# RetNet attention and a top-2 expert layer on one core: where evacuations, fetches and a loop count are issued

## The chip, the core and the metric

The kernel runs on one core of a Trainium2 chip. A core has five engines that run their own instruction queues in order: TensorE (PE; its weight loads are shown as PEld), VectorE (DVE), ScalarE (ACT), GpSimd (POOL) and SyncE (SP, which here only issues DMAs). They wait for one another through semaphores. Matmul results land in PSUM and must be copied ("evacuated") to SBUF by DVE or ACT before the PSUM buffer can be used again. The metric is the device time of one execution in microseconds (us), as a median of runs. All times below are in us unless marked ns, and places in the run are given from the start of the span, which reaches from the first to the last instruction.

## The reference

Attention with a decay in place of a softmax feeds a mixture of eight experts of which each token takes two.

```
scores = scale * q @ k.T                      # q, k, v: (8, 8, 576, 64)
ret    = scores * Dmat                        # Dmat: gamma_h ** (i - j) for i >= j, else 0
attn   = ret @ v
x = attn.transpose(0, 2, 1, 3).reshape(4608, 512)
logits = x @ w_gate + log1p(exp(x @ w_noise)) * noise
top2, weights = the two largest logits of a token, softmax over the two
out[token] = sum over its two experts of weight * (relu(x @ w1[e]) @ w2[e])   # w1: 512x1024, w2: 1024x512
```

## The kernel before

**Attention** works in 16 units. Unit u is one batch and four heads; two batches (bp) make four units. 512 of the 576 positions are done with 128-wide tiles, and the last 64 ("the tail") of two batches together. The methods of the class Attention (the main loop's order in a unit is scores for hp 0, out, tr of q, scores for hp 1, cast and tr of k, scores_tail, states and out_tail, with one step() behind each of these seven):
- scores(u, hp) (L248): 16 matmuls of keys and queries into two PSUM tiles "S" (two buffers), then the evacuation: DVE multiplies them with the causal mask into two tiles S in bf16 (L263). It is called for hp 0 and hp 1.
- out(p) (L290) for the unit before: 32 matmuls of S with the values (L305) and 6 with the carried states and queries (L313) into two PSUM tiles "x"; one is copied to xT by ACT (L321) and one by DVE (L319).
- tr(u+1, "q") and tr(u+1, "k") (L228): 8 transposes each into PSUM "tr" (two buffers, shared with the router's row copies), and a copy by ACT to QT or KT (L244).
- cast(u+2) (L185): POOL scales k and q into kn (L192) and qb (L200), ACT casts v (L197).
- scores_tail, states(u) (L266: 32 matmuls into PSUM "T", one buffer, copied by ACT to Tb, L285), out_tail.

**The router** is a Python generator, route(bp) (L469), for the tokens of two batches. It is cut into pieces by yield. The inner function step() of the main function runs one piece; the main loop calls it seven times a unit, between the calls above, so that a piece's instructions stand in every engine's queue between those of attention. One route spreads over four units. Its pieces are: the logits matmuls (L489) and the first row of x (transposes L482, copy L483); the logits to SBUF (lg, L496 and L497) and exp and ln of the noise part on ACT (L499, L500, with an ACT table load); noise and the first maximum (L515 to L525); the second maximum; the choice M, running counts cum on POOL (L549) and exp of the difference d (L553); gates, ranks and flags (L558 to L636); one-hot products olo and oh on DVE (L643 to L652, two halves); two groups of nine matmuls R (L663), one for each half; then the table of slots (L667 and finish(), L690 to L693), a matmul of counts (L681), and the end. The rows of x go to DRAM as xd (L626).

**The early tiles.** When three routes are done, early() (L354) starts on five tiles of expert work, again piece by piece, beside the last route: gathers on POOL (L370), transposes (L383), first and second matmuls (L392, L402).

**The experts.** experts() handles the other 35 tiles of 256 tokens (LATE, expert by expert). The order of instructions is written out by hand. In iteration i: the results of tile i-1 that are a token's first expert are scaled and stored to yd (fin); tile i+2 is transposed (L931, copied by ACT L934); the second matmuls of tile i (L966) are issued two by two with the first matmuls of tile i+1 (L947), whose evacuations to hT alternate between ACT (L952) and DVE (L954); comb(i-1), issued behind the second of these evacuations, adds the scaled result of tile i-1 to prv, which holds the rows of yd from the token's other expert (L1002). Then, on POOL: gathers of tile i+5 (L828), and for each half s of a tile the scatter of tile i-1 to out (L1008) and the fetch prev(i+1, s) of rows of yd (L974). Last come casts and loads of weights. The second matmuls run over the contraction index outside and the two halves inside, so both halves of a tile end together. prv has four buffers.

**The end.** After all scatters POOL copies keep["nov"], the number of overflow tiles, to keep["nov2"] (L1055); this copy waits for every row of out. overflow() then loads that count into a register of each engine (L739) and enters a loop (L740), which runs as often as the count says.

Of the kernel before, what the change touches and what calls it, by code (L numbers as in the profile page):

```python
# [9 lines left out]
F32 = mybir.dt.float32  # L10
# [119 lines left out]
class Attention:  # L130
# [3 lines left out]
    def __init__(self, tc, ctx, raw, K, q, k, v):  # L134
        self.tc, self.nc, self.K = tc, tc.nc, K
        self.src = dict(q=q, k=k, v=v)
        nc = self.nc
        ep = lambda n, b, **kw: ctx.enter_context(tc.tile_pool(name=n, bufs=b, **kw))
        self.cp = ep("at_c", 1)
        self.raw = raw  # L140
        self.bf = ep("at_bf", 2)
        self.tp = ep("at_t", 2)
        self.sp = ep("at_s", 2)
        self.xp = ep("at_x", 2)
        self.ps = ep("at_ps", 1, space=bass.MemoryType.PSUM)
        self.Tb = [self.cp.tile([P, 2, 4, P], BF16, name=f"Tb{j}") for j in range(4)]
        self.u = {}
        self.tails = {}
        self.T = {}
        self.xT = {}  # L150

    @staticmethod
    def unit(u):

        return u // 4, u // 2 % 2, u % 2

    def tables(self):
# [90 lines left out]
    def scores(self, u, hp):  # L248
        nc = self.nc
        d = self.u[u]  # L250
        p = [self.ps.tile([P, 2, 2, P], F32, name="S", bufs=2) for h in range(2)]
        for c in range(2):
            for r in range(2):
                for h in range(2):
                    s = slice(h * HD, (h + 1) * HD)
                    for e in range(2):
                        nc.tensor.matmul(p[h][e * HD:(e + 1) * HD, c, r, :],  # L257
                                         lhsT=d["K"][s, hp, c, r, e, :],
                                         rhs=d["Q"][s, hp, 2 * c + e, :],
                                         start=(c == 0 and r == 0), stop=(c == 1 and r == 1), skip_group_check=True)  # L260
        for h in range(2):
            S = self.sp.tile([P, 2, 2, P], BF16, name=f"S{hp}{h}")
            nc.vector.tensor_tensor(S, p[h], self.K["mask"].unsqueeze(1).to_broadcast([P, 2, 2, P]), Alu.mult)  # L263
            d["S", hp, h] = S

    def states(self, u):  # L266
# [15 lines left out]
        T = self.Tb[u % 4]  # L282
        for h in range(2):
            s = slice(h * HD, (h + 1) * HD)
            nc.scalar.activation(T[s, :, :, s].rearrange("p y n d -> p (y n) d"),  # L285
                                 p[s].rearrange("p y n d -> p (y n) d"), Act.Copy)
        for hp in range(2):
            d["T", hp] = self.T[bp, b, 2 * hq + hp] = T[:, hp]

    def out(self, u):  # L290
# [17 lines left out]
        for e in range(2):  # L308
            for hp in range(2):
                for c in range(2):  # L310
                    j = 2 * c + e
                    if j:
                        nc.tensor.matmul(p[e][:, hp, c, :],  # L313
                                         lhsT=d["T", hp][:, j - 1, :], rhs=d["Q"][:, hp, j, :], start=False,
                                         stop=(hp == 1 and c == 1), skip_group_check=True)
            xv = self.xT[bp][:, 2 * hq:2 * hq + 2, 4 * b:4 * b + 4, :].rearrange(
                "p y (c e) t -> p y c e t", e=2)[:, :, :, e, :]
            if e:
                nc.vector.tensor_copy(xv, p[e])  # L319
            else:  # L320
                nc.scalar.activation(xv, p[e], Act.Copy)  # L321

# [109 lines left out]
class Router:  # L432
# [36 lines left out]
    def route(self, bp):  # L469
# [26 lines left out]
        V.tensor_copy(lg, pg[:, :, 1])  # L496
        V.tensor_add(lg, lg, pg[:, :, 0])  # L497
        nl = sp.tile([P, C, E], F32, name="nl")
        nc.scalar.activation(nl, lg[:, :, E:], Act.Exp)  # L499
        nc.scalar.activation(nl, nl, Act.Ln, bias=1.0)  # L500
        yield
        row(1)
# [48 lines left out]
        d = col("d")  # L551
        V.tensor_sub(d, m2, m1)  # L552
        nc.scalar.activation(d, d, Act.Exp)  # L553
        yield

# [102 lines left out]
        G.tensor_tensor(key, key, ov, Alu.mult)  # L658
        G.tensor_scalar(key, key, -1.0, None, Alu.add)
        pT = ps.tile([P, 2 * NH], F32, name="R", bufs=1)  # L660
        for j in range(2):
# [70 lines left out]

def overflow(tc, K, w1, w2, keep, xd, yd, out):

    nc = tc.nc
    V = nc.vector
    with tc.tile_pool(name="ov_c", bufs=1) as cp, tc.tile_pool(name="ov_o", bufs=4) as op, \
         tc.tile_pool(name="ov_ps", bufs=1, space=bass.MemoryType.PSUM) as ps:
        n = nc.values_load(keep["nov2"][0:1, 0:1], min_val=0, max_val=NOV)  # L739
        with tc.For_i(0, n, 1) as iv:  # L740
            kb = cp.tile([P, 1], F32, name="kb")
            V.tensor_copy(kb, keep["ovk"][:, bass.ds(iv, 1)])
            e = nc.gpsimd.value_load(keep["ove"][0:1, bass.ds(iv, 1)], min_val=0, max_val=E - 1)
# [89 lines left out]
def experts(tc, K, wp, w1, w2, keep, xd, yd, out, W, pre):  # L833
# [7 lines left out]
    with tc.tile_pool(name="moe_g", bufs=1) as gp, \  # L841
# [117 lines left out]
        def g2(i):  # L959
            w = W[LATE[i][0]]  # L960
            hT = st[i]["hT"]
            po = [ps.tile([P, DM], F32, name="po", bufs=4) for s in range(2)]
            for fi in range(KF):
                for s in range(2):
                    o = KD * F + fi * DM
                    nc.tensor.matmul(po[s], lhsT=hT[:, fi, s * P:(s + 1) * P], rhs=w[:, o:o + DM],  # L966
                                     start=(fi == 0), stop=(fi == KF - 1))
                    yield
            st[i]["po"] = po

        def prev(i, s):
            if i < NT and seconds(i)[s]:
# [3 lines left out]
                    in_offset=IOff(ap=st[i]["ix"][:, s, 1:2], axis=0),  # L976
                    bounds_check=rows - 1, oob_is_err=False)

        def fin(i):
# [35 lines left out]
        with tc.manual_schedule(engines=order):  # L1015
# [9 lines left out]
            for _ in g1(0, {}):  # L1025
                pass
            wload(0)
            for i in range(NT + 1):
                if i:
# [14 lines left out]
                for s in range(2):  # L1044
                    if i + 5 < NT:
                        gather(tc, keep, xd, xgof(i + 5), i + 5, s)
                for s in range(2):
                    if i and seconds(i - 1)[s]:
                        scat(i - 1, s)
                    prev(i + 1, s)  # L1050
                st.pop(i - 1, None)
                wcast(i)
                wload(i + 1)

        last = nc.gpsimd.tensor_copy(keep["nov2"], keep["nov"]).ins  # L1055
        for w in writes:
# [15 lines left out]
def kernel(  # L1072
# [20 lines left out]
    keep = dict(z=cp.tile([P, NH], F32, name="z"), xi=cp.tile([P, NH], I32, name="xi"),  # L1093
                key=cp.tile([P, 2, NCOL], F32, name="key"), nov=cp.tile([P, 1], I32, name="nov"), nov2=cp.tile([P, 1], I32, name="nov2"),
                ovk=cp.tile([P, NOV], F32, name="ovk"), ove=cp.tile([P, NOV], I32, name="ove"))
# [4 lines left out]
    with ExitStack() as actx, tc.manual_schedule(engines=order):  # L1100
# [131 lines left out]
```

## Time and profile before

| what | us |
|---|---|
| median of 6 runs | 580.49 (578.16 to 584.46) |
| the profiled execution | 578.05 |
| its span | 576.3 |
| PE busy | 450.2 (78%) |
| DVE busy | 272.6 (47%) |
| ACT busy | 275.1 (48%) |
| POOL busy | 287.0 (50%) |
| mean granted TensorE clock | 0.858 of full speed |

A busy share is a mean over stretches with different limits, so the run is best read in stretches: loading and the first units (0 to 48), attention with routes (48 to 186), the last route with the early tiles (186 to 245), the experts (245 to 557), and the end. In the lines of the profile a group is named by its line in the kernel, engine, operation and tiles (out<-in), and the bracket holds the idle time of the engine just before it and what ended that. "issue" stands for idle time that the profile cannot lay to another engine.

### The profile page before, as it was taken

Reading aid. Unit: us, or ns where it says so; the run is one execution under the profiler, and the core shown is the slowest. Engines: PE = TensorE matmul, PEld = TensorE weight load, DVE = VectorE, ACT = ScalarE, POOL = GpSimd, SP = SyncE. Lnnn points to the kernel's source line nnn. Section 1 sums busy time; section 2 is a strip of 40 time slices with the busy share of each in tenths; the row PEclk is TensorE's granted clock in tenths of the full one; section 3 lists DMA queues with packets and bytes.
Section 4 is the critical chain, followed back from the end, with each engine's and each line's share of the span. In section 5 each row is a group of like instructions: output and inputs, shape, how many; then the busy total and the mean of one; then the engine's idle time right before and its main releaser. Section 6 shows DMA issues by size and latency. Waiting matters only on the chain.

```text
span 576.3 us, 11679 instructions
## 1 busy us (share of the span) xinstructions
PE 450.2 (78%) x4587; PEld 312.9 (54%) x4627; DVE 272.6 (47%) x696; ACT 275.1 (48%) x413; POOL 287.0 (50%) x377
## 2 busy tenths in 40 slices
PE   1697776884783799689996996997996997898960
PEld 1576554663562566466662663664563664465630
DVE  5354997698577485333231351341332333243430
ACT  4686963782581585436553652753452642212200
POOL 4962495278333555721464055157067165576470
PEclk9987775676686799799996998998799899899995
DMA  9976999606717224636684676667565643443350
GB/s 262 346 187 185 288 347 279 201 28 136 125 32 149 76 83 150 190 138 221 208 276 151 208 242 203 222 238 235 200 221 179 225 145 118 140 144 124 126 183 20
DMA packets 96169, 104.19 MB, mean 181 GB/s; under 512 B 25447, under 2 KB 73064, under 8 KB 96112
## 3 DMA queue, kind: packets, MB, share of 16 engines
q1 hardware_dynamic: 79824, 69.51, 38.0%
q0 software_dynamic: 14176, 32.83, 20.4%
q10 hardware_dynamic: 2112, 1.08, 0.6%
q8 instruction: 37, 0.61, 0.4%
q14 instruction: 20, 0.16, 0.1%
HBM read 84.66 MB, written 28.72 MB: 197 GB/s over the span
## 4 chain that ended last, share of the span: by engine, by line
PE 35%; issue 22%; DVE 16%; POOL 10%; DMA 7%; SPq 4%; ACT 2%; another core or an unknown queue 1%; POOLq 0%; DVEq 0%; ACTq 0%
PE p L947 12%; PE po L966 10%; POOL xg L828 4%; DVE S L263 3%; SPq L174 2%; PE S L392 2%; DMA xg<-xd,xi 2%; DMA raw_k<-in_k_dram 2%; PE x L402 2%; POOL prv L974 2%; DMA raw_q<-xd,xi 2%; POOL out_dram L1008 2%; DVE olo L643 1%; PE T L279 1%
## 5 line engine op out<-in xcount | busy, mean ns | idle before, releaser
L947 PE MATMUL p<-xgT,w 128*128 128x256 bf16 x1120 | 222.6, 282 | 22.1 <-issue 15.7
L966 PE MATMUL po<-w,hT 128*128 128x512 bf16 x525 | 204.1, 393 | 9.5 <-issue 7.0
L947 PEld LDWEIGHTS <-w 128*128 128x128 bf16 x1120 | 112.5, 101 | 102.6 <-issue 35.9
L954 DVE TENSOR_SCALAR hT<-p 128x512 bf16<-128x512 f32 x70 | 48.3, 691 | 195.2 <-PE p L947 119.2
L952 ACT ACTIVATE hT<-p 128x512 bf16<-128x512 f32 x70 | 41.8, 598 | 171.1 <-PE p L947 63.7
L1008 POOL DMA_INDIRECT out_dram<-o,ix x45 | 45.6, 1013 | 114.2 <-DVE o L1002 100.0
L828 POOL DMA_INDIRECT xg<-xd,xi x64 | 65.8, 1028 | 19.2 <-issue 17.4
L966 PEld LDWEIGHTS <-hT 128*128 128x128 bf16 x560 | 55.9, 100 | 23.4 <-issue 15.3
L974 POOL DMA_INDIRECT prv<-yd,ix x45 | 46.0, 1023 | 36.1 <-DMA wst<-in_moe_w_dram 22.7
L263 DVE TENSOR_TENSOR S<-S,mask 128x512 bf16<-128x512 f32 x64 | 41.1, 684 | 32.8 <-PE S L257 32.6
L897 ACT ACTIVATE w<-wst 128x1024 bf16<-128x1024 f32 x48 | 47.9, 1050 | 0.0
L192 POOL TENSOR_TENSOR kn<-raw_k,kg 128x1024 bf16<-128x1024 f32 x14 | 27.2, 1940 | 29.3 <-PE T L279 15.4
L934 ACT ACTIVATE xgT<-pt 128x1024 bf16<-128x1024 bf16 x35 | 35.7, 1020 | 2.2 <-PE pt L931 2.2
L1002 DVE SCALAR_TENSOR_TENSOR o<-po,g,prv 128x512 f32<-128x512 f32 x45 | 31.7, 743 | 3.0 <-DMA prv<-yd,ix 3.0
L200 POOL TENSOR_TENSOR qb<-raw_q,qg 128x1024 bf16<-128x1024 f32 x14 | 30.3, 2165 | 0.0
L257 PE MATMUL S<-QT,KT 64*64 64x128 bf16 x512 | 19.1, 278 | 10.3 <-DVE S L263 7.1
L549 POOL TENSOR_TENSOR cum<-cum,M 128x16 bf16<-128x16 bf16 x36 | 8.1, 226 | 36.5 <-DVE d L552 34.0
L242 PE MATMUL tr<-ident,qb 128*128 128x128 bf16 x128 | 15.3, 292 | 12.8 <-DVE qb L200 12.8
L279 PE MATMUL T<-vn,kn 64*64 64x64 bf16 (+2 forms) x512 | 25.3, 243 | 0.0
L482 PE MATMUL tr<-ident,xT 128*128 128x128 bf16 x144 | 17.6, 260 | 9.5 <-ACT QT L244 7.5
L483 ACT ACTIVATE xr<-tr 128x512 bf16<-128x512 bf16 x36 | 21.4, 597 | 4.6 <-issue 2.9
L931 PE MATMUL pt<-ident,xg 128*128 128x128 bf16 x256 | 20.7, 219 | 3.0 <-issue 2.5
(210 smaller groups left out, 659.0 us busy)
## 6 DMA issues: line engine op xcount, KB each, us to landing
wst<-in_moe_w_dram SPq DMA_DIRECT2D x48, 512.0 KB
raw_k<-in_k_dram SPq DMA_DIRECT2D x32, 256.0 KB
raw_v<-in_v_dram SPq DMA_DIRECT2D x32, 256.0 KB
yd<-y SPq DMA_DIRECT2D x16, 512.0 KB
raw_q<-in_q_dram SPq DMA_DIRECT2D x14, 512.0 KB
xd<-xr SPq DMA_DIRECT2D x12, 396.0 KB
w<-in_moe_w_dram POOLq DMA_DIRECT2D x4, 1024.0 KB
yd<-raw_v SPq DMA_DIRECT2D x5, 512.0 KB
```

The source lines that it names most:

```text
L263: nc.vector.tensor_tensor(S, p[h], self.K["mask"].unsqueeze(1).to_broadcast([P, 2, 2, P]), Alu.mult)
L279: nc.tensor.matmul(p[h * HD:(h + 1) * HD, hp, n, :], lhsT=d["kn"][:k, r, c, 2 * hp + h, :], rhs=m, start=(c == 0 and k == P and r == 0 and ...
L828: tc.nc.gpsimd.indirect_dma_start(out=xg[:, s, :], out_offset=None, in_=xd[:, :], in_offset=IOff(ap=keep["xi"][:, j:j + 1], axis=0), bound ...
L897: nc.scalar.activation(W[e][:, k * F:(k + 1) * F], t, Act.Copy)
L934: return lambda: nc.scalar.activation(xgT, pt, Act.Copy)
L947: nc.tensor.matmul(p1[:, f2, :], lhsT=w[:, o:o + P], rhs=xgT[:, di, :], start=(di == 0), stop=(di == KD - 1))
L952: nc.scalar.activation(hT[:, 2 * fp:2 * fp + 2, :], p1, Act.Relu)
L954: V.tensor_relu(hT[:, 2 * fp:2 * fp + 2, :], p1)
L966: nc.tensor.matmul(po[s], lhsT=hT[:, fi, s * P:(s + 1) * P], rhs=w[:, o:o + DM], start=(fi == 0), stop=(fi == KF - 1))
L974: nc.gpsimd.indirect_dma_start(out=prv[i % NP][:, s, :], out_offset=None, in_=yd[:rows, :], in_offset=IOff(ap=st[i]["ix"][:, s, 1:2], axis=0),
L1002: V.scalar_tensor_tensor(o[:, s, :], st[i]["po"][s], st[i]["g"][:, s:s + 1], prv[i % NP][:, s, :], Alu.mult, Alu.add)
L1008: ins = nc.gpsimd.indirect_dma_start(out=out[:, :], out_offset=IOff(ap=st[i]["ix"][:, s, 0:1], axis=0), in_=st[i]["o"][:, s, :], in_offset ...
```

## The change

It has these parts.
1. The evacuations in scores, states and out are put into small functions, kept in a list self.late, and issued by flush(), which step() calls after the router piece. So the evacuation of a call stands behind the router piece that follows it, in the queues of DVE and ACT. Both copies of xT are issued together. scores_tail, out_tail and tr are as before.
2. In route, two yields move: the one behind exp and ln of the noise part now stands ahead of them, and the one behind exp of d now stands ahead of it. One yield is added ahead of the two R groups, so a route has one piece more.
3. In experts, the fetches of y of a tile are issued up to two tiles ahead (i+2 in iteration i), both halves together and ahead of the scatters, as soon as stored() says that all tiles whose rows they can read have had their stores issued.
4. In the last tile the second matmuls run half by half: all eight of the first half, then all eight of the second.
5. The loop count is read ahead of experts(), straight from keep["nov"]; the copy that waits for the rows of out now copies keep["ovk"] (96 columns) to keep["ovk2"], which the loop reads.

```diff
@@ class Attention
+    def flush(self):
+
+        for f in self.late:
+            f()
+        self.late.clear()
@@ scores
-        for h in range(2):
-            S = self.sp.tile([P, 2, 2, P], BF16, name=f"S{hp}{h}")
-            nc.vector.tensor_tensor(S, p[h], self.K["mask"].unsqueeze(1).to_broadcast([P, 2, 2, P]), Alu.mult)
-            d["S", hp, h] = S
+
+        def take():
+            for h in range(2):
+                S = self.sp.tile([P, 2, 2, P], BF16, name=f"S{hp}{h}")
+                nc.vector.tensor_tensor(S, p[h], self.K["mask"].unsqueeze(1).to_broadcast([P, 2, 2, P]), Alu.mult)
+                d["S", hp, h] = S
+        self.late.append(take)
@@ states: the copies to T likewise
...
@@ out
-            xv = self.xT[bp][:, 2 * hq:2 * hq + 2, 4 * b:4 * b + 4, :].rearrange(
-                "p y (c e) t -> p y c e t", e=2)[:, :, :, e, :]
-            if e:
-                nc.vector.tensor_copy(xv, p[e])
-            else:
-                nc.scalar.activation(xv, p[e], Act.Copy)
+
+        def take():
+            xv = self.xT[bp][:, 2 * hq:2 * hq + 2, 4 * b:4 * b + 4, :].rearrange("p y (c e) t -> p y c e t", e=2)
+            nc.scalar.activation(xv[:, :, :, 0, :], p[0], Act.Copy)
+            nc.vector.tensor_copy(xv[:, :, :, 1, :], p[1])
+        self.late.append(take)
@@ route
         V.tensor_add(lg, lg, pg[:, :, 0])
+        yield
         nl = sp.tile([P, C, E], F32, name="nl")
         nc.scalar.activation(nl, lg[:, :, E:], Act.Exp)
         nc.scalar.activation(nl, nl, Act.Ln, bias=1.0)
-        yield
         row(1)
...
         V.tensor_sub(d, m2, m1)
+        yield
         nc.scalar.activation(d, d, Act.Exp)
-        yield
...
         G.tensor_scalar(key, key, -1.0, None, Alu.add)
+        yield
         pT = ps.tile([P, 2 * NH], F32, name="R", bufs=1)
@@ overflow
-        n = nc.values_load(keep["nov2"][0:1, 0:1], min_val=0, max_val=NOV)
         with tc.For_i(0, n, 1) as iv:
             kb = cp.tile([P, 1], F32, name="kb")
-            V.tensor_copy(kb, keep["ovk"][:, bass.ds(iv, 1)])
+            V.tensor_copy(kb, keep["ovk2"][:, bass.ds(iv, 1)])
@@ experts, g2
-            for fi in range(KF):
-                for s in range(2):
+
+            for fi, s in ((fi, s) for fi in range(KF) for s in range(2)) if i + 1 < NT else (
+                    (fi, s) for s in range(2) for fi in range(KF)):
@@ experts
+        def stored(i, n):
+
+            return i >= NT or all(j < n for j in range(NT) if LATE[j][0] < LATE[i][0] and any(firsts(j)))
...
+            pv = 0
             for i in range(NT + 1):
...
+                while pv <= i + 2 and stored(pv, i):
+                    for s in range(2):
+                        prev(pv, s)
+                    pv += 1
                 for s in range(2):
                     if i and seconds(i - 1)[s]:
                         scat(i - 1, s)
-                    prev(i + 1, s)
...
-        last = nc.gpsimd.tensor_copy(keep["nov2"], keep["nov"]).ins
+        last = nc.gpsimd.tensor_copy(keep["ovk2"], keep["ovk"]).ins
@@ main function, step
                     work.append(early(tc, K, at, keep, xd, yd, W, EARLY, routed))
+            at.flush()
             if n == NU:
                 more()
@@ main function, end
+    nov = nc.values_load(keep["nov"][0:1, 0:1], min_val=0, max_val=NOV)
     experts(tc, K, wp, moe_w1, moe_w2, keep, xd, yd, out, W, pre)
-    overflow(tc, K, moe_w1, moe_w2, keep, xd, yd, out)
+    overflow(tc, K, moe_w1, moe_w2, keep, xd, yd, out, nov)
```

More of the change, by code (lines that the diff above doesn't have):

```diff
@@ L146, in __init__ @@
         self.Tb = [self.cp.tile([P, 2, 4, P], BF16, name=f"Tb{j}") for j in range(4)]
+        self.late = []
         self.u = {}
@@ L282, in states @@
         T = self.Tb[u % 4]
[L283 to L286, printed above, removed]
+        def take():
+            for h in range(2):
+                s = slice(h * HD, (h + 1) * HD)
+                nc.scalar.activation(T[s, :, :, s].rearrange("p y n d -> p (y n) d"),
+                                     p[s].rearrange("p y n d -> p (y n) d"), Act.Copy)
+        self.late.append(take)
         for hp in range(2):
@@ L315, in out, with take @@
                                          stop=(hp == 1 and c == 1), skip_group_check=True)
-            xv = self.xT[bp][:, 2 * hq:2 * hq + 2, 4 * b:4 * b + 4, :].rearrange(
-                "p y (c e) t -> p y c e t", e=2)[:, :, :, e, :]
-            if e:
-                nc.vector.tensor_copy(xv, p[e])
-            else:
-                nc.scalar.activation(xv, p[e], Act.Copy)
+        def take():
+            xv = self.xT[bp][:, 2 * hq:2 * hq + 2, 4 * b:4 * b + 4, :].rearrange("p y (c e) t -> p y c e t", e=2)
+            nc.scalar.activation(xv[:, :, :, 0, :], p[0], Act.Copy)
+            nc.vector.tensor_copy(xv[:, :, :, 1, :], p[1])
+        self.late.append(take)
     def scores_tail(self, bp, hq):
@@ L730, in overflow_list, with overflow @@
         V.scalar_tensor_tensor(keep["ovk"], self.K["iota"][:, :NOV], float(P), ei, Alu.mult, Alu.add)
-def overflow(tc, K, w1, w2, keep, xd, yd, out):
+def overflow(tc, K, w1, w2, keep, xd, yd, out, n):
     nc = tc.nc
@@ L1093 @@
     keep = dict(z=cp.tile([P, NH], F32, name="z"), xi=cp.tile([P, NH], I32, name="xi"),
-                key=cp.tile([P, 2, NCOL], F32, name="key"), nov=cp.tile([P, 1], I32, name="nov"), nov2=cp.tile([P, 1], I32, name="nov2"),
+                key=cp.tile([P, 2, NCOL], F32, name="key"), nov=cp.tile([P, 1], I32, name="nov"), ovk2=cp.tile([P, NOV], F32, name="ovk2"),
                 ovk=cp.tile([P, NOV], F32, name="ovk"), ove=cp.tile([P, NOV], I32, name="ove"))
```

## The prediction

> **What bounds the kernel now.** I read the page first (its share by engine and its chain), then the busy times by stretch, then the waits of each engine in the attention stretch, then the timelines at the places that these named. All times are microseconds from the start of the span. The span is 576.3, the profiled execution took 578.05, so 1.75 lie around it; the median of the runs shown is 580.49, which is 2.44 above the profiled execution. I make the sum against 578.05 and add the 2.44 at the end.
>
> ```profile
> 48.00:186.00 138.00, 96.12 (x1721) 75.44 (x1720) 107.75 (x249) 79.94 (x119) 71.47 (x105) 0.67 0.69 175
> 245.00:300.00 55.00, 52.31 (x391) 36.49 (x397) 19.10 (x57) 28.43 (x38) 18.22 (x19) 0.99 0.61 209
> 480.00:557.00 77.00, 69.04 (x473) 44.72 (x481) 32.06 (x81) 19.79 (x29) 45.90 (x46) 0.98 0.41 134
> 557.00:576.30 19.30, 0.00 (x0) 0.00 (x0) 1.06 (x2) 0.00 (x0) 4.03 (x5) 0.58 0.20 70
> ```
>
> Columns are the stretch, its length, busy time of PE, PEld, DVE, ACT and POOL, the granted clock, DMA share and GB/s. There are three regimes. From 48 to 186 attention and router share the engines: DVE is busy 78%, no engine is full, so waits between engines decide. From 245 to 557 PE is full (95% in the first of the two stretches shown): there the order of DMAs on POOL costs nothing unless PE runs dry. From 557 PE is done and POOL's queue alone sets the end. So the change is worth something in the first regime and the last.
>
> ```profile
> PE R L663 <- DVE oh L652: 14.8, 6, 4.6
> PE tr L482 <- ACT QT L244: 7.5, 3, 2.9
> PE S L257 <- DVE S L263: 6.9, 4, 3.2
> ```
>
> These are PE's three longest waits of 48 to 186 (total, times, longest). The first two are the router's pieces getting into attention's way, and the change moves both.
>
> **Evacuations behind the router piece: the end of a group.** Four units of attention carry one route. A group takes 48 to 49 (the lg copies stand at 57.08, 105.05 and 154.09). At its end the second half of the one-hot products is made while PE waits in order for it:
>
> ```profile
> 138.25 1.65 DVE L650 TENSOR_TENSOR oh<-oh,cols 128x720 bf16<-128x720 bf16 x1
> 139.94 1.95 DVE L652 TENSOR_SCALAR oh<-oh,pidx 128x720 bf16<-128x720 bf16 x1
> 141.94 1.36 PE L663 MATMUL R<-oh,olo 128*128 128x160 bf16 x9 [4.65 <-DVE oh L652]
> 143.23 0.64 PE L257 MATMUL S<-QT,KT 64*64 64x128 bf16 x16
> 143.91 1.29 DVE L263 TENSOR_TENSOR S<-S,mask 128x512 bf16<-128x512 f32 x2 [1.43 <-PE S L257]
> 145.48 0.17 PE L681 MATMUL R<-cum,ones 128*128 128x16 bf16 x1 [1.61 <-DVE L L667]
> ```
>
> Read it downward: DVE ends its product at 141.89, PE does the second R group, then the score matmuls, DVE idles 1.43, and PE waits again 1.61 before the transposes of kn. In the changed instruction lists R moves one piece later (the new yield), so the scores of the unit's second half stand before that second R, and the S evacuation of the first half stands behind the products. DVE has the same work up to 141.89, in another order. Then: scores at 141.9 to 142.2 (they follow the freed buffers), R 1.36 to 143.5, transposes of kn at 143.5 instead of 145.50; the counts matmul falls behind them and no longer stalls. That is 2.0 a group. From 146 to 154 PE runs without a gap over 0.3, so the 2.0 stay. Two groups end with scores behind them (at 94 and 142; the first shows the same wait, 4.38); the third has none. **Gain 4.0.**
>
> **Yields moved in the router's first pieces.** Before, ScalarE's table load stood ahead of the QT copy:
>
> ```profile
> 154.76 0.26 ACT L499 ACTIVATE nl<-lg 128x72 f32<-128x72 f32 x1 [1.11 <-DVE lg L497]
> 155.04 1.28 ACT L500 ACT_TABLE_LOAD   x1
> 156.50 1.01 ACT L244 ACTIVATE QT<-tr 128x1024 bf16<-128x1024 bf16 x1
> 157.56 0.58 PE L482 MATMUL tr<-ident,xT 128*128 128x128 bf16 x4 [2.88 <-ACT QT L244]
> ```
>
> After, QT is first (154.15, when its transposes end, to 155.17), then exp, table load and ln (0.26+1.28+0.26, to 156.97), then the xr copy of 0.6 to 157.55; the kn transposes, which need that copy's buffer, come at 157.55 instead of 158.05. So 2.88 of wait is worth only 0.5: the wait moves from the row's transposes to kn's. Three groups: **1.5**. This adds a wait: the nl product now stands in the next DVE slot, waits for ln until 157.0, and the S evacuation of 154.72 stands behind it, until 157.6 to 158.9. Who waits for that? The next scores, at 160.99; they do not, by 2.1. The exp of d moves likewise; its load (113.89) already ran in a pause of ACT. DVE then fills the 0.42 for which it waits for PE before the xT copy (114.35 and 163.66) with the 0.65 of pd and thr: 0.4 twice, **0.8**. The Tb copies go behind a row copy of 0.6; their reader (L313) comes 2.7 after the copy's end (149.92 to 152.62), so nothing.
>
> **The start of the early tiles.** One more piece per route makes early begin one step later, and the instruction lists have the tail's products and the first logits matmuls (1.01 and 0.72) ahead of its first transposes. These waited 4.11 for a gather (184.56 to 188.67), so 1.7 of PE work goes into that wait. What is late next is the copy to raw_v (190.58 to 191.6), beside which the next 16 logits matmuls and a row (0.63 and about 0.4) stand. The second R of the last route has the same number of early pieces ahead of it as before. **1.7.**
>
> **The experts.** The pairs of fetches of y now go out one tile earlier and ahead of the scatters; their number is the same (45 at 1.02 each). POOL's queue behind a fetch that waits for its stored rows holds the scatters and then the gathers. Before, one fetch waited 22.7 (248.4 to 271.1) and PE stood nowhere over 0.5 between 251 and 302: a gather is issued two whole tiles before its transposes, some 15 at 7.6 a tile (379.63 to 387.21). Later the scatters themselves wait for DVE up to 22.5, so POOL is ahead. **0**, with up to 7 lost if one 22.7 wait came back where POOL leads by only 15 (its wait at 357 and at 403).
>
> **The end.**
>
> ```profile
> 555.52 1.03 POOL L974 DMA_INDIRECT prv<-yd,ix  x1 [0.30 <-issue]
> 559.05 0.75 DVE L1002 SCALAR_TENSOR_TENSOR o<-po,g,prv 128x512 f32<-128x512 f32 x1 [1.74 <-DMA prv<-yd,ix]
> 560.78 0.98 POOL L1008 DMA_INDIRECT out_dram<-o,ix  x1 [0.30 <-issue]
> 563.74 0.19 POOL L1055 COPY nov<-nov 128x1 int32<-128x1 int32 x1 [1.97 <-DMA out_dram<-o,ix]
> ```
>
> From 551.54 POOL issues eight DMAs, one each 1.31; the last two fetches lie between. After, the order is six scatters: 551.54, 552.86, then 554.93 (its o starts at 553.93, first half 0.7, handover 0.3), 556.25, 557.57, 558.88. The o of the last tile's first half can start at 555.4, since with halves in order its 8 matmuls end at about 554.9; the second half's o runs from 556.9 to 557.65. The last scatter is at 558.88 instead of 560.78: **1.9**. By scatter spacing alone it would be 2.6, without the halves about 1.2.
>
> The loop count: the lists show the load moved only on SP. On PE, ACT, DVE and POOL it still stands last, and POOL's own comes behind the copy, which still waits for every row of out. What it waits for is done earlier, but POOL's queue is what ends. Gain 0 (at best the 0.5 of one load). SP now waits for nov (230.68) between two stores of y; at most 1, and the weights behind it went out at 238.04. The copy is 96 wide instead of 1: rows near it are 0.17 (128x24) and 0.56 (128x528 memset), I take 0.1 **lost**.
>
> **Sum.** 4.0 + 1.5 + 0.8 + 1.7 + 1.9 - 0.1 = 9.8. 578.05 - 9.8 = 568.25, and on the median 570.7.
>
> **Two costs that the trace of before cannot fix.** First, the same DVE instruction takes 1.75 or 0.23 (L602), 1.95 or 0.43 (L652), 1.77 or 0.18 (L636), the long ones whenever POOL casts kn or qb beside it, and S evacuations do not stretch. A new order meets other casts: one collision of 1.5 more or less in each of three groups, so 4.5 either way; I take 0. [...] Second, the granted clock was 0.50 from 133.3 to 153.8. If PE's shorter waits released it, the 8 of full PE work from 146 to 154 could shrink by up to half, 4 a group; the clock can equally stay, so 0 is taken. [...]
>
> **Rivals.**
> (1) Bonus: as forecast, and collisions or the clock give 4 to 9 more: 562 to 567. For it: S evacuations, which do not collide, now face the second cast. Against: DVE, not PE, is bound from 116 to 142. Chance 0.16.
> (2) Given back: the new wait behind ln (2.9 in three groups, 8.7) is paid, and eats the 8.0 of attention and start; 1.8 at the end remain: about 579.4. It decides if the next scores come less than 2.9 after the old evacuation's end; the row says 5.0 (156.0 to 160.99). Chance 0.17.
> (3) Slower: every S evacuation behind a router piece is waited for by PE's next scores, since there are two buffers. Pieces ahead in a group: 2.9 (nl), 0.8 (w, M), 0.9 (r, df), 1.2 (rki to ov), 0.9 (oh), 1.3 (the products), 8.0, three groups 24.0, less 9.8: 594.7. It decides where the delay passes the spare time between an evacuation and the next scores: 2.2 (113.77 to 115.94) and 4.3 (117.86 to 122.18), but nothing where PE already waits 2.92 (131.75), where DVE is the bound anyway. Chance 0.15.
> (4) The change not doing what it says concerns the loop count alone, and is in the sum at 0.
>
> **How the numbers follow.** The forecast, 570.7, has 0.52; its own range is 564 to 577. With rival 1 that is 0.68 for faster by over 0.5% (below 577.6); 0.5% is about what a measurement of this kernel can tell from no change. Within: 0.17. Slower: 0.15. The range of 8 in 10 runs from 562 (9.8, 4.5 and 4 all gained) to 582 (rival 2 with 2.6 of collisions) and leaves out rival 3.
>
> **What would show it.** Right: no PE wait of over 2 at L663's second group of the first two routes; QT ahead of the table load; groups of 45 to 46.5; stretch 245 to 557 as long as before; six scatters at the end. Wrong: S evacuations with PE's scores waiting for them over 10 in total; a fetch of y waiting over 15; a later last scatter in relation to the last matmul.

## The result and the profile after

The changed kernel takes **586.35** in the median of 20 runs (583.64 to 593.47), the kernel before 580.57 (46 runs). The ratio is 1.0095, with a 95% interval of 1.0075 to 1.0114: about 1% slower, where 570.7 was forecast and 582 was the range's end. The profiled execution took 585.19, its span 583.5.

Line numbers from the class Attention on are 7 to 22 higher in the changed kernel: L263 is L272 there, L257 L264, L244 L251, L523 L536, L652 L665, L663 L677, L1008 L1026.

Busy time by stretch, after (columns as in the prediction):

```profile
48.00:186.00 138.00, 95.44 (x1794) 75.57 (x1795) 108.13 (x242) 83.34 (x125) 65.81 (x105) 0.71 0.75 179
245.00:300.00 55.00, 48.16 (x360) 34.51 (x366) 15.91 (x47) 28.57 (x38) 16.77 (x17) 0.91 0.60 206
557.00:583.50 26.50, 8.83 (x53) 5.04 (x52) 5.43 (x8) 1.19 (x2) 6.13 (x7) 0.74 0.17 66
```

From 245 to 300 PE is busy 48.16 in place of 52.31, since the experts begin later (their first xgT copy stands at 251.0 in place of 240.6); in the last row PE still works after 557. So everything stands later, and the time is lost before the experts. PE's longest waits from 48 to 186, after:

```profile
PE S L264 <- DVE S L272: 21.1, 15, 6.5
PE S L264 <- ACT KT L251: 5.7, 2, 3.9
PE tr L249 <- ACT xr L496: 5.3, 3, 1.8
...
PE R L677 <- DVE oh L665: 1.3, 2, 1.1
PE tr L495 <- ACT QT L251: 1.1, 2, 0.5
```

The two waits that the change was to remove are gone (R from 14.8 to 1.3, row transposes from 7.5 to 1.1). The wait for QT moved to the transposes of kn, which wait for the xr copy (5.3), as forecast. But the waits for S evacuations went from 6.9 to 21.1; over 10 was to speak against the forecast. The end of a group shows the exchange (timeline, after):

```profile
140.39 1.28 DVE L272 TENSOR_TENSOR S<-S,mask 128x512 bf16<-128x512 f32 x2
141.12 0.32 PE L264 MATMUL S<-QT,KT 64*64 64x128 bf16 x2 [4.75 <-DVE S L272]
...
148.90 0.43 DVE L665 TENSOR_SCALAR oh<-oh,pidx 128x720 bf16<-128x720 bf16 x1
149.24 1.27 DVE L272 TENSOR_TENSOR S<-S,mask 128x512 bf16<-128x512 f32 x2
149.97 0.32 PE L264 MATMUL S<-QT,KT 64*64 64x128 bf16 x2 [2.72 <-DVE S L272]
...
151.13 1.38 PE L677 MATMUL R<-oh,olo 128*128 128x160 bf16 x9
```

The second R group (151.13) now waits for nothing, but the scores wait 4.75 and 2.72 for evacuations that stand behind router pieces, and 4.65 was the wait removed.

To see where the rest lies, I cut each span at four landmarks: the first lg copy (loads and first units), the first xgT copy of the experts, the last xgT copy, and the end. These are the profiles that the text below uses, all from one execution each ("aligned" means that tiles keep their place within 256 bytes, "no deferral" that evacuations are issued at once; both are told below):

| kernel | to first lg | to first xgT | experts | end | span |
|---|---|---|---|---|---|
| before | 57.1 | 183.5 | 301.2 | 34.6 | 576.3 |
| after | 60.7 | 190.3 | 299.9 | 32.6 | 583.5 |
| e1 attention as before | 64.9 | 183.5 | 298.3 | 33.0 | 579.7 |
| e5 before, shifted by 352 bytes | 64.3 | 180.9 | 302.5 | 34.6 | 582.3 |
| e6 after, aligned | 56.0 | 185.7 | 289.5 | 33.0 | 564.2 |
| e7 no deferral, aligned | 56.9 | 178.1 | 288.4 | 32.9 | 556.3 |
| e8 attention as before, aligned | 59.5 | 184.5 | 293.1 | 33.3 | 570.5 |
| e16 before, shifted by 512 bytes | 58.8 | 180.9 | 253.5 | 34.6 | 527.8 |
| e14 as e7 | 58.1 | 174.0 | 252.6 | 33.2 | 517.8 |
| e17 as e6 | 54.8 | 180.1 | 253.0 | 33.3 | 521.2 |

Against before, the changed kernel loses 3.6 at the start and 6.8 in attention, and gains 1.3 in the experts and 2.0 at the end. From e13 on every kernel was 45 to 49 quicker, the kernel before too (528 in place of 577; told last), so each result is given as a ratio to the kernel before measured beside it.

### The profile page after: what moved, and what is told of

The parts are those of the page before. It is cut to its first block, busy times and chain, and to the rows that moved or that the text cites. A ratio compares the mean times of both kernels' runs of the same rounds, so it can differ in the third digit from the quotient of the medians.

```text
span 583.5 us, 11684 instructions
## 1 busy us (share of the span) xinstructions
PE 451.4 (77%) x4587; PEld 312.9 (54%) x4627; DVE 274.0 (47%) x696; ACT 274.9 (47%) x413; POOL 279.0 (48%) x377
## 4 chain that ended last, share of the span: by engine, by line
PE 52%; DVE 18%; issue 10%; DMA 6%; SPq 5%; ACT 3%; another core or an unknown queue 3%; POOL 1%; POOLq 0%; DVEq 0%; ACTq 0%
PE p L960 23%; PE po L980 19%; DVE S L272 3%; DMA raw_v<-in_v_dram 3%; PE pt L944 3%; SPq L181 3%; PE S L405 2%; PE x L415 2%; SPq L188 2%; DVE olo L656 1%; DVE o L1020 1%; DVE oh L663 1%; DVE oh L660 1%; PE R L677 1%
## 5 line engine op out<-in xcount | busy, mean ns | idle before, releaser
L1026 POOL DMA_INDIRECT out_dram<-o,ix x45 | 45.6, 1013 | 113.8 <-DVE o L1020 99.9
L272 DVE TENSOR_TENSOR S<-S,mask 128x512 bf16<-128x512 f32 x64 | 41.1, 683 | 31.9 <-PE S L264 31.6
L264 PE MATMUL S<-QT,KT 64*64 64x128 bf16 x512 | 20.3, 268 | 28.2 <-DVE S L272 21.3
L947 ACT ACTIVATE xgT<-pt 128x1024 bf16<-128x1024 bf16 x35 | 35.7, 1019 | 5.5 <-PE p L960 3.2
L264 PEld LDWEIGHTS <-KT 64*64 64x64 bf16 x512 | 12.8, 130 | 33.5 <-issue 23.8
L207 POOL TENSOR_TENSOR qb<-raw_q,qg 128x1024 bf16<-128x1024 f32 x14 | 28.1, 2005 | 0.0
L204 ACT ACTIVATE vn<-raw_v 128x1024 bf16<-128x1024 f32 x16 | 16.9, 1056 | 17.6 <-DMA raw_v<-in_v_dram 11.8
L249 PE MATMUL tr<-ident,qb 128*128 128x128 bf16 x128 | 13.8, 273 | 12.8 <-DVE qb L207 12.8
L496 ACT ACTIVATE xr<-tr 128x512 bf16<-128x512 bf16 x36 | 21.1, 596 | 4.4 <-PE tr L495 2.7
```

The source lines that it names most:

```text
L264: nc.tensor.matmul(p[h][e * HD:(e + 1) * HD, c, r, :], lhsT=d["K"][s, hp, c, r, e, :], rhs=d["Q"][s, hp, 2 * c + e, :], start=(c == 0 and ...
L947: return lambda: nc.scalar.activation(xgT, pt, Act.Copy)
L1026: ins = nc.gpsimd.indirect_dma_start(out=out[:, :], out_offset=IOff(ap=st[i]["ix"][:, s, 0:1], axis=0), in_=st[i]["o"][:, s, :], in_offset ...
```

## The experiments

**Which part loses.** Theory A: the new wait for ln is paid (rival 2). Theory B: every S evacuation behind a piece is late (rival 3). Theory C: the loss has to do with neither. e1 undoes the attention and router parts (the two xT copies stay together), e2 only the deferral:

```diff
-        self.late.append(take)     # e1, e2: in scores, states and out
+        take()
```

> The changed kernel with the attention and router parts undone: evacuations at once, all three yields in their old places; the fetches of y, the last tile half by half and the loop count stay. Theory A (the nl product waits for ln, and the S evacuation behind it, 8.7 in three groups) and theory B (every S evacuation behind a router piece is late for PE's next scores): both lay the loss to the undone parts, so what is left is the end, 2.0 faster than before: ratio to before 0.9965, about 578.5. Theory C (the stalls at the start, +2.8, and ahead of the experts, +4.6, come of the parts that stay, such as the loop count's load): about 583 to 586, ratio 1.005 to 1.01.

Measured: 1.0141 (0.998 to 1.0302).

> The changed kernel with the evacuations of scores, states and out issued at once; the three yields, the experts, the end and the loop count as changed. Theory A and theory B: no S evacuation stands behind the nl product or any other piece, so the loss goes: end 2.0, R yield up to 4.0 and the other yields up to 1.5 gained: 573 to 577, ratio 0.987 to 0.994. If a yield by itself does the damage (an instruction queued behind the nl product other than S, as the kn or xT copies): 581 to 586. Theory C: 581 to 586, with the stall ahead of the experts still there.

Measured: 1.0024 (0.9942 to 1.0105). e3 puts one yield of the changed kernel back, e4 all three:

```diff
         V.tensor_add(lg, lg, pg[:, :, 0])
-        yield
         nl = sp.tile([P, C, E], F32, name="nl")
         nc.scalar.activation(nl, lg[:, :, E:], Act.Exp)
         nc.scalar.activation(nl, nl, Act.Ln, bias=1.0)
+        yield
         row(1)
```

> The changed kernel with only the yield at exp and ln of the noise part put back behind them. Theory A: the wait of DVE for ln (8.0 in three groups in the profile of after) goes, and with it most of the loss: 578 to 580, ratio about 0.997. Theory B: the S evacuations still stand behind the other pieces; at most the 1.5 that this yield was to gain is lost as well: 585 to 588, ratio 1.007 to 1.012. Theory C: 585 to 588.

Measured: 1.0071 (1.0019 to 1.0122).

> The changed kernel with all three yields as before: the deferral alone, beside the experts, the end and the loop count. Theory A: no nl product waits for ln, the gain at a group's end (3.2 to 4.0) is gone, the end's 2.0 stays: about 578 to 580, ratio 0.997. Theory B: the deferral alone costs PE its waits for DVE's S evacuations (21.1 in 48 to 192 against 6.9): 586 to 592, ratio 1.010 to 1.02. Theory C: 583 to 588.

Measured: 1.005 (0.9927 to 1.0173). No kernel of the four was shown to be faster than before (the intervals of e1, e2 and e4 include 1), not even e1, in which little but the end is left of the change; A and B alone had it at 0.9965. In e1 attention took 183.5, as before, and the end was 1.6 shorter, but the first lg copy came at 64.9 in place of 57.1; in the other three at 61.9 to 64.2. So something that all of them share slows the start, where the loads set the pace (from 8 to 62 POOL waits most for raw_k, 12.8 in all in before and 16.2 in e1). What they share is one line that I had passed over (it isn't in the diff shown above):

```diff
-  nov2=cp.tile([P, 1], I32, name="nov2"),
+  ovk2=cp.tile([P, NOV], F32, name="ovk2"),      # NOV = 96
```

The tile grows from 4 to 384 bytes in a partition, and every tile that is laid out behind it moves by 352 bytes: raw_q, where q lands, from 53504, a multiple of 256, to 53856, 96 past one.

**The address alone (theory D).** e5, e9 and e16 are the kernel before with nov2 widened to 96, 104 and 136 columns (shifts of 352, 384 and 512 bytes). e6, e7 and e8 are the changed kernel, e2 and e1 with ovk2 padded to 136 columns, a shift of 512, which keeps the place within 256.

```diff
-  ovk2=cp.tile([P, NOV], F32, name="ovk2"),
+  ovk2=cp.tile([P, 136], F32, name="ovk2")[:, :NOV],
```

> The kernel before, in which the tile of the loop count is given 96 columns in place of 1 (only the first is used), as wide as the tile that the change puts there. Every tile that is laid out behind it moves by 352 bytes, the DMA destinations too: raw_q from 53504 (a multiple of 256) to 53856 (96 past one). Nothing else differs. Theory D (the address costs time: in the profiles of the changed kernel and of the two without deferral a 512-byte packet of the first loads took 32 ns against 27, a 1024-byte one 53 against 46, and the loads of 8 to 16 moved 290 GB/s against 346): the first lg copy comes at 61 to 65 in place of 57.1, and the whole is 4 to 8 slower, ratio 1.007 to 1.014. Theories A and B (the loss is in the order of the instructions): 1.000 and packets of 27 ns. Theory C in its other form (noise of placement): no telling, and no change of the packets.

Measured: 1.0098 (1.0053 to 1.0143), first lg copy at 64.3.

> The kernel before with the loop count's tile 104 columns wide: all later tiles move by 384 bytes, raw_q to 53888, which is a multiple of 64 and 128 past a multiple of 256. Theory D1 (the place within 256 bytes counts): at least as slow as the shift by 352, since a row of 512 bytes now touches three pieces of 256 in place of two as well: 512-byte packets of the first loads at 32 to 34 ns, the first lg copy at 61 to 66, ratio 1.007 to 1.016. Theory D2 (only the place within 64 bytes or less counts): 27 ns, 57 to 59, ratio 1.000. [...]

Measured: 1.0156 (1.009 to 1.0222), first lg copy at 63.1.

> The kernel before with the loop count's tile 136 columns wide: every later tile moves by 512 bytes and keeps its place within 256. Theory D1: nothing changes, packets of 512 bytes at 27 ns, the first lg copy at 55 to 60, ratio 0.998 to 1.002. If any shift costs time: 61 to 65 and 1.007 to 1.016, as for 352 and 384.

Measured: 0.9987 (0.9964 to 1.001), first lg copy at 58.8. The loads from 8 to 16 as rows of busy time by stretch (the last column is GB/s, the one ahead of it the DMA share), first of the kernel before:

```profile
8.00:16.00 8.00, 1.98 (x20) 1.72 (x24) 6.79 (x20) 3.14 (x4) 6.42 (x14) 1.00 1.20 291
```

After:

```profile
8.00:16.00 8.00, 1.99 (x20) 1.73 (x24) 6.79 (x20) 3.15 (x4) 6.42 (x15) 1.00 1.26 245
```

e5:

```profile
8.00:16.00 8.00, 1.99 (x20) 1.72 (x24) 6.79 (x20) 3.15 (x4) 6.41 (x15) 1.00 1.27 245
```

e16:

```profile
8.00:16.00 8.00, 1.99 (x20) 1.72 (x24) 6.79 (x20) 3.15 (x4) 6.41 (x14) 1.00 1.18 287
```

The queues are busier and move 15 to 16% less: each packet lasts longer. (The 346 and 290 GB/s in e5's expectation are the level from 8 to 11, ahead of a fall that both have.) By the trace's packet records (medians, 5 to 20) packets of 512 bytes take 27 ns where the shift is 0 or 512, and 32 at 352 and at 384 (means 31.6 to 31.8 and 32.4); those of 256 bytes 18 against 24 to 26; those of 1024 bytes 46 against 53 to 54. PE's first transposes of a tail, which wait for POOL's cast of it (qt), wait 2.4 to 2.7 in before, e16, e6, e7 and e17 and 5.2 to 6.3 in after, e1, e5 and e9. D holds, in the form D1: the shift by 384, a multiple of 64, costs as much, the shift by 512 nothing (245 and 248 GB/s from 8 to 16 at 352 and 384, 291 and 287 at 0 and 512). No run separates 256 from 512 as the unit, and none shows why a packet lasts longer; what was moved is the place in SBUF to which the loads write. At 384 the packets of 512 bytes took as long as at 352, 32, not the 34 at the end of e9's range.

> The changed kernel, its tile of the loop's keys padded to 136 columns, so that all later tiles move by 512 bytes against before and keep their place within 256. Theory D with the loss all there: the 4 to 8 of the start come back: 578 to 582 where the kernel before takes 580.5, ratio 0.996 to 1.003, packets of 27 ns. Theory A or B alone: no change against the changed kernel, ratio 1.008 to 1.011.

Measured: 0.9896 (0.985 to 0.9943), first lg copy at 56.0, faster than the 0.996 to 1.003 expected. Without the shift **the change is a gain**; nothing else differs from the changed kernel, so the address turned it into a loss.

> The changed kernel with evacuations at once and the three yields as changed, padded to the same 512 bytes. The profile without the padding stood 3.7 below the one of before, with 7.0 lost ahead of the first lg copy. Theory D: both are had, 7 to 11 below before: ratio 0.981 to 0.988. Without D: as without the padding, 0.994 to 1.0.

Measured: 0.982 (0.9744 to 0.9896).

> Experts, last tile and loop count as changed, attention and router as before, padded to the same 512 bytes. Theory D: the first lg copy is back at 57 to 58, and the end's 1.7 to 2.0 is all that differs from before: ratio 0.996 to 0.998. Without D: as without the padding, 1.005 to 1.014.

Measured: 0.9943 (0.9885 to 1.0), first lg copy at 59.5. The three pairs give 2.0% for the shift (1.0095 and 0.9896; 1.0024 and 0.982; 1.0141 and 0.9943), but the halves of a pair were not measured together. e5 and e9, each beside the kernel before, give 1.0 and 1.6%. The start explains some 4 to 7 of 580, about 1%. Most of the rest of the pairs' difference lay in the experts, 5 to 10 by the profiles, and I tested whether their addresses matter, too.

**The experts.** e13 is e7 with a tile of 352 bytes ahead of the experts' tiles, so that only they are displaced; e14 is e7 again, beside it; e15 is e7 with the fetches of y in the old order.

```diff
+        gap = gp.tile([P, 88], F32, name="gap")     # e13
+        nc.vector.memset(gap[:, :1], 0.0)
         xgs = [gp.tile([P, 2, XW], F32, name=f"xg{j}") for j in range(NX)]
```

> Evacuations at once, padded to 512 bytes, but with 352 bytes of padding ahead of the experts' own tiles, so that these stand within 256 bytes where the changed kernel has them (wst, y, o and prv at 32 past a multiple in place of 192, the gathered rows at 96 in place of 0), and those of attention where before has them. If the address also slows the experts: their stretch (first to last xgT copy) 295 to 300, 5 longer than the control, ratio 0.988 to 0.993. If the experts' packets do not care (they last as long in all profiles so far) and the difference was scatter: 288 to 293 as the control, ratio 0.980 to 0.985.

Measured: 0.982 (0.9786 to 0.9853), experts 252.5.

> The kernel with evacuations at once, padded to 512 bytes, a second time, as the control of the runs beside it: ratio 0.980 to 0.985, experts 288 to 295. If its first profile was a lucky one, the experts take 295 to 301 here and the ratio is 0.986 to 0.99.

Measured: 0.981 (0.9784 to 0.9836), experts 252.6.

> As the control, with the fetches of y one tile ahead and behind the scatters, as before; the last tile half by half stays. If the early fetches shorten the experts: their stretch 299 to 303, as in the three profiles with the old order, and the ratio 0.990 to 0.996; also the last scatter comes about 0.7 later behind the last xgT copy. If they give nothing, as forecast: experts as in the control within 4, ratio 0.981 to 0.987.

Measured: 0.9848 (0.9824 to 0.9872), experts 252.4. So neither the experts' addresses nor the early fetches matter inside the experts, where PE's pauses (told last) are absent. The differences of 3 to 12 in the earlier runs are probably scatter of these pauses: e11 (told below), without the shift, took 301.5 there, as long as before. The fetches, with the last tile half by half, are worth 2.0 at the end, by the last scatter behind the start of PE's last matmul: 4.42 before, 4.40 in e15, 2.44 in e14 and after.

**What the deferral and the yields do, with the address right.** e10 is e6 with exp and ln ahead of the yield again, e12 is e8 with the R yield alone.

> The changed kernel with the padding to 512 bytes, and exp and ln of the noise part ahead of the yield again. Theory A (the cost of the deferral is the nl product that waits for ln with an S evacuation behind it): from the first lg copy to the first xgT copy of the experts 178 to 180 in place of 185.7, ratio 0.976 to 0.984. Theory B (every S evacuation behind a piece costs): 184 to 187, ratio 0.988 to 0.992.

Measured: 0.9851 (0.9736 to 0.9967), 184.7 to the first xgT copy in place of 185.7. By that stretch theory B holds: the wait for ln is 1.0 of the deferral's cost there; the ratio decides nothing.

> Evacuations at once, padded to 512 bytes; of the three yields only the one ahead of the R groups; experts, last tile and loop count as changed. If that yield gives 4.0 to 7 at the ends of the groups and loses 6 in the last route, as the segments say: from the first lg copy to the first xgT copy 181 to 185, ratio 0.990 to 0.996, and the other two yields are worth 3 to 5. If it is the source of nearly all that the yields gave (184.5 to 178.1): 178 to 180, ratio 0.980 to 0.985.

Measured: 0.9908 (0.9864 to 0.9952), 181.5. So in attention the R yield gives 3.0 (184.5 to 181.5) and the other two yields 3.4 more (178.1), and the deferral takes 7.6 away (185.7). These are single profiles, and those of before and e5, which share the order, lie 2.6 apart (183.5 and 180.9), so the split of the yields is rough. e17 repeats e6, in the company of e18, which repeats e11: the yield ahead of R only in the first three routes.

```diff
         G.tensor_scalar(key, key, -1.0, None, Alu.add)
-        yield
+        if bp < 3:
+            yield
```

> The changed kernel, padded to 512 bytes, a second time. If the deferral costs what the segments say (7.6 from the first lg copy to the first xgT copy): ratio 0.990 to 0.996, 8 to 9 below nothing but the padding's 12. If it costs nothing (the first difference was scatter of the experts): 0.979 to 0.984, as the kernel without it.

Measured: 0.9927 (0.9896 to 0.9957). The changed kernel without the shift is 0.7% faster than before, and without the deferral 1.9% (e14): the deferral costs 1.2%, some 6, and the two profiles differ by as much in attention (180.1 against 174.0).

> Evacuations at once, padded to 512 bytes, and the yield ahead of the two R groups taken only in the first three routes. Theory E (in the last route the added piece lets one more piece of the early tiles in ahead of the table, 51.8 in place of 45.7 from the last lg copy to the first xgT copy): 45 to 48 there and all else as with the yield in all routes: ratio 0.970 to 0.975. Rival (the 6 is work that was moved there from the group before, whose end became 3.2 shorter): 50 to 52 stays, ratio 0.981 to 0.984.

Measured: 0.9864 (0.9797 to 0.9931), 45.6 from the last lg copy to the first xgT copy: the stretch that theory E had, but not its ratio.

> The kernel with evacuations at once and the yield ahead of the R groups in the first three routes, padded, a second time. If the 3.6 ahead of the experts reaches the end: ratio 0.972 to 0.978. If the experts give it back, as in its first profile (301.5): 0.980 to 0.985.

Measured: 0.9881 (0.985 to 0.9911), outside both ranges, 46.1 there; e14, which has the yield in all routes, has 46.1 as well, and a better ratio. So the yield by itself does not make the 51.8 of e7, and theory E's gain does not reach the end. But up to e12 every kernel with the yield in all routes took 51 to 54 there, and every one without it in the last route 44 to 48; why that difference is gone from e13 on stays open. The best version measured is e14.

How does the deferral cost 6 if the waits only move? Busy time from 48 to 180, first of e16 (the order of before):

```profile
48.00:180.00 132.00, 91.43 (x1687) 72.34 (x1684) 100.78 (x234) 80.19 (x119) 70.76 (x104) 0.68 0.71 178
```

e14 (yields):

```profile
48.00:180.00 132.00, 90.93 (x1721) 72.73 (x1720) 106.23 (x248) 79.99 (x119) 70.98 (x104) 0.74 0.73 185
```

e17 (yields and deferral):

```profile
48.00:180.00 132.00, 91.31 (x1690) 72.45 (x1689) 106.19 (x239) 79.44 (x119) 65.10 (x104) 0.70 0.73 185
```

PE is busy as long in all three, but at a granted clock of 0.68, 0.74 and 0.70, and does fewer matmuls in the time (x1687, x1721, x1690). The stretches from the first to the last lg copy last 136.9, 127.9 and 133.6; in them PE stands idle 43.4, 40.3 and 40.6, is busy 93.5, 87.6 and 93.0, and the clock is halved for 92.5, 69.8 and 82.4. So e17 stands idle no longer than e14; nearly all of the 5.8 by which its stretch is longer is PE's busy time, 5.4. Of that time 62.9 in e17 and 53.9 in e14 lie at half clock, 9.0 more. In before, 16 score matmuls take 0.64 at half clock (143.23) and 0.42 at full (164.69), 8 transposes 1.06 (56.22) and 0.61 (68.97); at these ratios the 9.0 make 3.1 to 3.8 of the 5.4, an estimate. e17's longest wait for an S evacuation is 4.8 against 3.5 in e14, but which wait goes with a halved clock, if any does, was not tried, so that these waits act through the clock is a guess of mine that no run shows.

## Why the prediction was wrong

**The copy "96 wide instead of 1", 0.1 lost.** This is the step that failed. The copy itself took 0.26 in place of 0.19, as forecast. But I priced the instruction, not the tile that it writes to, whose size moves all that is laid out behind it. In the kernel before the same shift costs 1.0% (e5, 5.7), and in the changed kernel padding it away turns 1.0095 into 0.9896. No rival of mine had this mechanism; the start of the span, where it acts, was in none of my terms. The sizes do not quite close: 0.7% gained (e17) less 1.0% lost would be some 1.5 slower, and 5.8 was measured; the other 4 are not explained, and PE's pauses in the experts scatter by more than that.

**"Nothing where PE already waits", in rival 3.** This failed as well: the forecast put the deferral's own cost at nothing. Five waits in the second halves of the first two groups make 17.3 of the 21.1: 6.53 and 1.57, ended at 95.66 and 102.12, and 1.70, 4.75 and 2.72, ended at 133.08, 141.12 and 149.97. The evacuations that PE waits for there stand behind the router's pieces, the longest behind the flags and one-hot products. The order at the end of the group itself came as forecast (scores at 149.97, R without a wait at 151.13, transposes of kn at 152.31, 1.8 behind the end of DVE's work, where 1.6 was forecast and 3.6 the row of before). But PE had paid for it earlier in the same group.

**"Who waits for that? The next scores; they do not, by 2.1."** That held in two groups of three (timeline, after, the first group and then the third):

```profile
65.82 1.12 DVE L536 TENSOR_TENSOR nl<-nl,noise 128x64 f32<-128x64 f32 x1 [2.94 <-ACT nl L514]
...
66.87 1.88 DVE L537 TENSOR_TENSOR nl<-nl,noiset 128x8 f32<-128x8 f32 x1
...
68.93 1.28 DVE L272 TENSOR_TENSOR S<-S,mask 128x512 bf16<-128x512 f32 x2
...
69.67 0.32 PE L264 MATMUL S<-QT,KT 64*64 64x128 bf16 x2 [1.07 <-DVE S L272]
...
163.98 1.28 DVE L272 TENSOR_TENSOR S<-S,mask 128x512 bf16<-128x512 f32 x2
...
166.93 0.32 PE L264 MATMUL S<-QT,KT 64*64 64x128 bf16 x2
```

DVE waits for ln as forecast (2.94; 8.0 in three groups, 8.7 in rival 2). In the third group the scores come 1.7 behind the evacuation's end and wait for nothing; in the second it is the same (119.11 behind 117.44). In the first group they wait 1.07: there two products that run beside POOL's casts (kn at 64.96, qb at 66.82, 1.90 each), 1.12 and 1.88 where the same lines take 0.23 and 0.16 in the third, stand ahead of the evacuation. That is the collision that I had put at 0. Putting this yield back shortened the first group by 1.7 and the others by 0.2 at most where the address was right (e6 to e10), and the three by 3.2, 0.9 and 1.8 where it was not (after to e3). So rival 2 is a small part of the deferral's 6 to 7.6 by the first pair; the rest must lie with the other pieces, rival 3's mechanism, at a fraction of its 24. By one profile each, the deferral without the yields cost nothing (e4 182.6, e1 183.5), so it seems that yields and deferral take the same slack.

**The ends of groups, 4.0, and the yields, 2.3.** Right in size only, and only without the deferral: there the yields gave 6.4 (e8 to e7) and 6.9 (e16 to e14) in attention, and the first two groups took 46.7 and 44.5 (e14; 45 to 46.5 was forecast). Most of it was not the waits that I had counted. From the first to the last lg copy the stretch became 12.4 and 9.0 shorter, of which PE's idle time makes 3.5 and 3.1 and its busy time, with less half clock, 8.9 and 5.9; the clock I had put at 0 and in rival 1. The last route gave 6.0 and 2.1 back. The start of the early tiles, 1.7, was no gain of its own: in the last route e17 takes 46.5 from lg to xgT and e16 44.0, which uses up most of the 3.3 gained up to the last lg copy.

**The experts, 0.** Right: 253.5 and 253.0 (e16, e17).

**The end, 1.9.** Right: 4.42 to 2.44, 1.98. The halves without the early fetches give nothing (e15, 4.40); what they add to the fetches, 0.7 by the forecast, no run shows. POOL's last two steps, after:

```profile
567.94 0.98 POOL L1026 DMA_INDIRECT out_dram<-o,ix  x1 [0.30 <-issue]
571.13 0.26 POOL L1077 COPY ovk<-ovk 128x96 f32<-128x96 f32 x1 [2.20 <-DMA out_dram<-o,ix]
```

With the address kept the change would have come to 0.9896 or 0.9927 of before, 574.5 to 576.3 on the median forecast from: 4 to 6 above the forecast, about what the deferral costs. Without the deferral 0.981 or 0.982 would be 569.5 to 570.1, close to the 570.7, but in part by luck: PE's busy time, shorter by 5.9 up to the last lg copy (e16 to e14), made up for the 1.7 that was not had.

## What to carry to other kernels

Read a change for what it does to the layout before its instructions: a wider tile that is allocated early moves every DMA destination behind it, and destinations that were moved by 352 bytes cost 16% of the load rate here (245 GB/s in place of 291 from 8 to 16), a shift of 512 next to nothing (287), so pad such a tile. Where all variants share a loss that no reordering explains, compare the stretch in which nothing was reordered. Of two edits that may use the same slack, price the second with the first in place.

## What was not expected of the hardware

**The address effect did not show in the experts.** There packets of 2048 and 4096 bytes take 84 and 159 ns (medians, 250 to 530) whether their tiles stand 192 or 32 bytes past a multiple of 256 (before and after), and e13, where the gathered rows stand 96 past one in place of 0, shows no loss (experts 252.5, beside 252.6 in e14).

**PE's pauses.** In the experts before, PE stood still in clusters some 40 to 50 apart (from about 303, 349, 399, 438 and 478) with nothing that the profile could lay it to (waits of PE, 245 to 540, before):

```profile
PE p L947 <- issue: 15.7, 23, 1.7
PE po L966 <- issue: 7.0, 13, 1.0
...
PE pt L931 <- issue: 2.5, 5, 1.0
```

The same instructions in e16 (the kernel before, shifted by 512), from 245 to 500, have no such line:

```profile
PE pt L931 <- DMA raw_q<-xd,xi: 5.2, 2, 4.9
PE p L947 <- DVE hT L954: 1.6, 1, 1.6
```

PE's gaps in the experts are 35.7 and 9.5, its time at half clock 42.9 and 6.8, and the experts take 301.2 and 253.5. These 47.7 are nearly the whole difference between 577 and 528. What makes these pauses come and go stays open: the kernel before itself took 577 beside e12 and 528 beside e13. They are the likely reason why times of one kernel lay 10 apart in the runs up to e12.
